# Three attention batches as one chain of head pairs, with products with v for six tiles at a time

## The chip, the cores and the metric

The kernel runs on one core of a Trainium2 chip. A core has five engines that run side by side, each working through its own instructions in order: TensorE (PE in the profile: matrix products and transposes; its weight loads are listed as PEld), VectorE (DVE), ScalarE (ACT), GpSimd (POOL) and SyncE (SP, which here only issues transfers). The metric is the device time of one execution in microseconds; lower is better.

## The reference

Windowed attention with a bias by distance, followed by a mixture of four experts. Cut to what matters:

```python
# q, k, v: (4 batches, 8 heads, 768 positions, 64)
scores = q @ k.T / sqrt(64) - slope[head] * dist      # dist: distance in positions
scores = where(is_global | is_local, scores, -1e9)    # first 8 columns, and the 96 before a row
a = softmax(scores)
attn = a @ v
x = attn.transpose(0, 2, 1, 3).reshape(3072, 512)
p = domain_probs / domain_probs.sum(-1)
out = sum(p[:, e] * (relu(x @ w1[e]) @ w2[e]) for e in range(4))   # w1: 512x1024, w2: 1024x512
```

All of it is float32.

## The kernel before

**Batches and stages.** Batch 0's attention runs first and nearly alone. Then come the experts of batches 0 and 1 (functions `first` for x times w1 with ReLU, `second` for the product with w2), and between their steps, as a second stream of work, the attention of batches 1, 3 and 2. At the end the experts of batches 2 and 3 run together with no attention left (`late_batch`). The expert products split each float32 operand into a high and a low part and use a seven-product scheme on 2x2 blocks, so an expert unit is seven groups of six 384-column products (`pm<-xB,w1s`, `pm<-xT,w1s`) and six groups of six 512-column products (`pm<-w2s,h`). Their four PSUM banks `pm` come free only when VectorE, and for the first kind ScalarE too, has read them.

**One batch of attention.** Heads go in four pairs, in the order `PAIRS`. A pair has six query tiles of 128 rows. `prepare_q` and `prepare_k` transpose half a pair's q or k on TensorE (`pt<-ident,q`, `pt<-ident,k`) and split it into high and low. For q the ScalarE part (L340) and the VectorE part (L341) go to a tile `st_q`, and four transfers (L345 to L347) copy its two heads into both partition halves of `qd`, so that one product can use the high and the low part of k, stacked in `kd`. `scores` makes a tile's scores (`ps<-kd,qd`, four products), `softmax` works on VectorE and ScalarE (`pb`, `nmax`, `zsum`), `turn` transposes the weights (`pt<-ident,pb`, copied to `pT`), and `weigh` multiplies three tiles by v (`pt<-pT,v`, `pt<-pT,vg`; `vg` holds v shifted to the window of the tile before). `weigh`'s result is copied out of PSUM by ScalarE: to `x` for batches 1 and 2, and for batch 3 to a small tile `piece` that ScalarE then sends to DRAM (L493 to L495, `x_last<-piece`). The tile `piece` has one buffer.

**Steps.** A tile goes through scores, exponentials, division and transposes in consecutive calls of `flow` (L507), and after three finished tiles `weigh` is called. Each of the three batches is a generator of 53 steps: one for its loads, 12 for each pair, and 4 that empty the pipeline. The main loop (L1393 to L1395) takes a step at about every second expert step.

**What sets the order.** In this stage (`Ordered.on = False`) a scheduler at build time interleaves the two streams by priority and by when it thinks a buffer is free; on the chip the order on each engine is then fixed, with waits on semaphores. Buffer counts (L983 to L985) matter for that reason: `pt` has two PSUM banks, shared by the transposes and by `weigh`; `qd`, `nat` (natural q and k) and `natv` (natural v) have one buffer each. SP issues all loads and copies, in order as well, so a load that waits for a free buffer holds those behind it.

Of the kernel before, what the change touches and what calls it, by code (L numbers as in the profile page):

```python
# [10 lines left out]
F32 = mybir.dt.float32  # L11
# [176 lines left out]
def attn_moe_kernel(ctx: ExitStack, tc, q, k, v, n_global, n_local, domain_probs, w1, w2, out):  # L188
# [95 lines left out]
    class Pools:  # L284


        def __init__(self, stack, name, st, kd, qd, nat, natv, pb, ps, pt, px, early, side="left"):
            self.early = early

            def sbuf(part, bufs):  # L290
                return stack.enter_context(tc.tile_pool(name=f"{name}_{part}", bufs=bufs, side=side))

            def psum(part, bufs):
                return stack.enter_context(tc.tile_pool(name=f"{name}_{part}", bufs=bufs, space=PSUM))

            self.st, self.natv = sbuf("st", st), sbuf("natv", natv)
            self.kd, self.qd, self.nat, self.vg = sbuf("kd", kd), sbuf("qd", qd), sbuf("nat", nat), sbuf("vg", kd)
            self.pb, self.pT, self.small = sbuf("pb", pb), sbuf("pT", 4), sbuf("small", pb)
            self.ps, self.pt = psum("ps", ps), psum("pt", pt)

            self.px, self.pxname = (psum("px", px), "px") if px else (self.pt, "pt")
# [197 lines left out]
    def attention(b, A, early=False):  # L499


        x = xs[b] = None if b == B - 1 else xp.tile([P, NPAIR, S], F32, name="x")
        if x is None:
            xd[b] = dp.tile([P, NPAIR, S], F32, name="x_last")
        tiles, turned, ahead = [None] * 4, [], [None]

        def flow(new=None):  # L507

            one, two, three, four = tiles
            if new:  # L510
                if not early:
                    new["ps"] = scores(A, new["t"], gots[new["pr"]])
                elif new["t"] % 2 == 0:
# [5 lines left out]
            ready = len(turned) == TPH  # L519
            if ready and not early:  # L520
                weigh(A, turned, x, b)
            if three and not early:
                turn(A, three)
            softmax(A, one, two)
            if three and early:
                turn(A, three)
            if ready and early:
                weigh(A, turned, x, b)
            if ready:
# [6 lines left out]

        def prepare(nat, got):

            got["v"] = nat
            prepare_q(A, nat["q"], 0, got)  # L540
            yield 1
            prepare_k(A, nat["k"], 0, got)
            yield 1
            prepare_q(A, nat["q"], 1, got)
            yield 1
            prepare_k(A, nat["k"], 1, got)
            yield 1
            nat["vg"] = windows(A, nat["v"])
            yield 1
            yield 1  # L550
# [17 lines left out]
        if early:  # L568
            halves = [load(A, src, b, 0, n, 2) for n, src in (("q", q), ("k", k))]
            bias = biases(start_stack.enter_context(tc.tile_pool(name="setup", bufs=1)))  # L570
            next(bias)
            nats[0] = dict(zip(("q", "k"), (next(h) for h in halves)))
            for h in halves:
                next(h)
            nats[0]["v"] = next(load(A, v, b, 0, "v"))
            todo = [prepare_all(pr) for pr in PAIRS]
            next(bias)
            next(todo[0])
            start(PAIRS[1])
        else:  # L580
            start(0)
            yield
        for m, pr in enumerate(PAIRS):
            cur = gots[pr]
            if not early:
                prep = prepare(nats[pr], cur)
                for _ in range(3):
                    next(prep)
                    flow()
                    yield  # L590
            for t in range(NQT):
                if early:
                    if t == 2 and m + 2 < NPAIR:
                        start(PAIRS[m + 2])
                elif t in (1, 2, 3):
                    next(prep)
                    flow()
                    yield
                if t == NQT - 1 and not early and m + 1 < NPAIR:
                    start(PAIRS[m + 1])  # L600
                flow({"t": t, "pr": pr, **cur})
                if early:
                    if (m, t) in BIASES:
                        next(bias)
                    for _ in range(AHEAD[m][t]):
                        while todo and next(todo[0], 0) == 0:
                            todo.pop(0)
# [4 lines left out]

# [348 lines left out]
    with ExitStack() as start_stack:  # L961
        A = Pools(start_stack, "start", st=1, kd=2, qd=2, nat=2, natv=3, pb=4, ps=2, pt=3, px=1, early=True)
        for n, _ in enumerate(attention(0, A, early=True)):
# [20 lines left out]
        att_stack, "att", st=1, kd=1, qd=1, nat=1, natv=1, pb=2, ps=2, pt=2, px=0, early=False, side="right"  # L984
# [367 lines left out]
    count, span = 3 * (NPAIR * (6 + NQT) + 5), (LATE * 13 * per - 12) * 0.97  # L1352
# [4 lines left out]
    att = chain(attention(1, A), attention(3, A), attention(2, A))  # L1357
# [87 lines left out]
```

## Time and profile before

| | us |
|---|---|
| median of 3 runs | 1180.61 (1180.2 to 1181.75) |
| the profiled execution's own time | 1180.03 |
| its span, first to last instruction | 1178.2 |
| of it 84 to 665, where experts and the three batches of attention share the engines | 581 |

The profile comes from one execution, 0.6 us below the median of the runs. PE is listed as busy for 98% of the span. In the profile's instruction lists a matrix product's end is modelled, so products overlap on paper; the time that one really costs TensorE is the distance from its start to the next one's start. A float32 product with v appears as two records. The helper that records instructions has one line, L44, so groups are told apart by tiles.

### The profile page before, as it was taken

The numbers are of one execution on the slowest core, as the hardware profiler recorded it, in microseconds if no ns is written. First come the engines' busy times: TensorE is split into PE (matmuls) and PEld (weight loads), VectorE is DVE, ScalarE is ACT, GpSimd is POOL, SyncE is SP. The second block draws the span as 40 slices with busy tenths as digits, with TensorE's granted clock in tenths as the row PEclk, the third lists the DMA queues.
The fourth block names the chain that finished last, engine by engine and source line by source line (L and its number), as shares of the span: only waits on it lengthen the run. The fifth ranks groups of instructions, "written<-read, shape, count | busy, mean of one in ns | idle before, by whom it ended". The sixth has DMA issues, their size and how long they took to land.

```text
span 1178.2 us, 21209 instructions
## 1 busy us (share of the span) xinstructions
PE 1149.0 (98%) x7488; PEld 1063.7 (90%) x7488; DVE 839.0 (71%) x1923; ACT 610.0 (52%) x1588; POOL 598.2 (51%) x584
## 2 busy tenths in 40 slices
PE   7789999999999999999999999999999999999997
PEld 5579898998898988888898889999999999999997
DVE  7876677676668677667666677777777777777776
ACT  6864767774743555455455434444444544444443
POOL 5776446455341222410420437777767855555554
PEclk9899999999999999999999999999999999999999
DMA  9578887886889899987897858888888687767764
GB/s 192 164 239 272 274 254 260 252 288 226 248 312 288 282 287 261 274 268 224 276 271 230 285 190 323 293 310 301 297 296 296 226 300 252 251 235 256 255 218 130
DMA packets 185201, 305.09 MB, mean 259 GB/s; under 512 B 87168, under 2 KB 137344, under 8 KB 172672
## 3 DMA queue, kind: packets, MB, share of 16 engines
q1 hardware_dynamic: 181488, 298.15, 77.8%
q10 hardware_dynamic: 3600, 5.51, 1.3%
q8 instruction: 62, 1.02, 0.4%
q14 instruction: 51, 0.42, 0.1%
HBM read 209.24 MB, written 70.78 MB: 238 GB/s over the span
## 4 chain that ended last, share of the span: by engine, by line
PE 87%; DVE 4%; DMA 3%; ACT 3%; issue 1%; POOL 1%; SPq 0%; DVEq 0%; ACTq 0%; POOLq 0%
PE pm L44 39%; PE pf L44 19%; PE X L44 11%; PE Y L44 9%; PE pt L44 6%; PE ps L44 3%; DMA qd<-st_q 2%; ACT pb L44 1%; DVE pb L44 1%; DMA raw<-in_moe_w_dram 1%; DMA out_dram<-acc 1%; POOL w1s L44 0%; DVE hA L44 0%; ACT pT L44 0%; SPq L44 0%
## 5 line engine op out<-in xcount | busy, mean ns | idle before, releaser
L44 PE MATMUL pm<-w2s,h 128*128 128x512 f32 x1152 | 288.4, 398 | 2.8 <-DVE h L44 2.8
L44 PEld LDWEIGHTS pm<-w2s,h 128*128 128x128 f32 x1152 | 209.6, 188 | 45.1 <-DVE h L44 3.9
L44 ACT ACTIVATE hf<-pf 128x384 f32<-128x384 f32 x128 | 62.8, 492 | 248.2 <-DVE pf L44 247.0
L44 POOL TENSOR_TENSOR hS<-sf,hS 128x384 fp32r<-128x384 f32 x126 | 133.5, 1077 | 112.9 <-ACT hS L44 112.2
L44 DVE SCALAR_TENSOR_TENSOR acc<-pm,prob,acc 128x512 f32<-128x512 f32 x180 | 133.7, 748 | 63.6 <-PE pm L44 62.5
L44 POOL TENSOR_TENSOR sums<-raw 128x256 f32<-128x256 f32 x54 | 39.2, 744 | 262.8 <-DMA raw<-in_moe_w_dram 183.2
L44 PE MATMUL pm<-xT,w1s 128*128 128x384 f32 x768 | 153.8, 341 | 0.7 <-DVE h L44 0.7
L44 PE MATMUL pf<-xT,w1s 128*128 128x384 f32 x768 | 146.5, 335 | 0.7 <-ACT hf L44 0.5
L44 PEld LDWEIGHTS pm<-xT,w1s 128*128 128x128 f32 x768 | 132.6, 188 | 3.2 <-DVE h L44 1.0
L44 PEld LDWEIGHTS pf<-xT,w1s 128*128 128x128 f32 x768 | 131.3, 188 | 1.5 <-ACT hf L44 1.0
L44 DVE TENSOR_TENSOR hA<-hf,hA 128x384 fp32r<-128x384 f32 x94 | 84.6, 925 | 50.5 <-ACT hA L44 50.5
L44 ACT ACTIVATE pb<-pb,nmax 128x256 f32<-128x256 f32 (+1 forms) x192 | 93.6, 493 | 46.9 <-DVE nmax L44 46.3
L44 PE MATMUL pm<-xB,w1s 128*128 128x384 f32 x570 | 115.5, 340 | 0.6 <-ACT x L44 0.6
L44 PE MATMUL pf<-xB,w1s 128*128 128x384 f32 x576 | 110.8, 335 | 0.1
L44 PEld LDWEIGHTS pm<-xB,w1s 128*128 128x128 f32 x570 | 98.7, 188 | 4.2 <-issue 1.4
L44 ACT ACTIVATE h<-pm 128x384 fp32r<-128x384 f32 x128 | 61.5, 489 | 73.8 <-DVE pm L44 72.5
L44 PEld LDWEIGHTS pf<-xB,w1s 128*128 128x128 f32 x576 | 98.7, 188 | 0.6 <-ACT hf L44 0.3
L44 POOL TENSOR_TENSOR sf<-hf 128x384 f32<-128x384 f32 x63 | 70.4, 1118 | 43.7 <-ACT hf L44 43.7
L44 DVE CUSTOM_DVE_ANT_0 pb<-ps,nbias 128x256 f32<-128x256 f32 (+1 forms) x192 | 71.4, 396 | 9.0 <-PE ps L44 8.2
L44 DVE SCALAR_TENSOR_TENSOR h<-pm,h 128x384 fp32r<-128x384 f32 x128 | 69.8, 551 | 8.4 <-ACT h L44 7.3
L44 PE MATMUL X<-w2b,hS 128*128 128x256 f32 x576 | 74.0, 282 | 0.0
L44 PE MATMUL Y<-w2b,hS 128*128 128x256 f32 x576 | 73.9, 282 | 0.0
(148 smaller groups left out, 2163.6 us busy)
## 6 DMA issues: line engine op xcount, KB each, us to landing
w1s<-kept SPq DMA_DIRECT2D x48, 1792.0 KB, 8.6
w2b<-kept SPq DMA_DIRECT2D x224, 256.0 KB, 4.1
kept<-w1s SPq DMA_DIRECT2D x16, 1792.0 KB, 9.8
raw<-in_moe_w_dram SPq DMA_DIRECT2D x43, 512.0 KB, 5.8
qd<-st_q SPq DMA_DIRECT2D x96, 192.0 KB, 3.8
kept<-w2s SPq DMA_DIRECT2D x16, 1024.0 KB, 7.0
w2s<-kept SPq DMA_DIRECT2D x16, 1024.0 KB, 6.6
v<-in_v_dram SPq DMA_DIRECT2D x16, 384.0 KB, 4.9
```

Of the source, the lines that this page charges most:

```text
L44: ins = fn(*args, **kwargs)
```

## The change

The second attention generator is written anew. Batch 0's (`attention_early`) is the old code with the other branch taken out. The other three batches become one generator, `attention_chain`, over twelve (batch, pair) items: the pipeline is no longer emptied between batches, and there are 149 steps in place of 159, spread over the same expert steps. `prepare_q` writes its high and low parts straight to the head's own half of `qd` (two ScalarE and two VectorE instructions on 64 partitions each) and copies each to the other half with one transfer. `weigh` is called twice in a row when six tiles have gathered. q and k of the next pair are requested at tile 2, v of the current pair right after the weighing of the pair before. `qd` gets two buffers and `pT` six (in `Pools`, for this stage alone).

```diff
-            self.pb, self.pT, self.small = sbuf("pb", pb), sbuf("pT", 4), sbuf("small", pb)
+            self.pb, self.pT, self.small = sbuf("pb", pb), sbuf("pT", 4 if early else 6), sbuf("small", pb)
...
         tp = transpose_half(A, nat, hf)
-        st = A.st.tile([P, 2, HALF], F32R, name="st_q")
-        ac.activation(st[:, 0, :], tp[:, :HALF], AF.Copy, scale=-SCALE)
-        ve.scalar_tensor_tensor(
-            st[:, 1, :], tp[:, :HALF], -SCALE, f32(st[:, 0, :]), op0=ALU.mult, op1=ALU.subtract
-        )
         qd = got[("q", hf)] = A.qd.tile([P, 2, 2, HALF], F32R, name="qd")
         for j in range(2):
-            for n in range(2):
-                sy.dma_start(f32(qd[n * D : (n + 1) * D, j]), f32(st[j * D : (j + 1) * D]))
+            own = slice(j * D, (j + 1) * D)
+            ac.activation(qd[own, j, 0], tp[own, :HALF], AF.Copy, scale=-SCALE)
+        for j in range(2):
+            own, oth = slice(j * D, (j + 1) * D), slice((1 - j) * D, (2 - j) * D)
+            ve.scalar_tensor_tensor(
+                qd[own, j, 1], tp[own, :HALF], -SCALE, f32(qd[own, j, 0]), op0=ALU.mult, op1=ALU.subtract
+            )
+            sy.dma_start(f32(qd[oth, j]), f32(qd[own, j]))
...
+    def attention_chain(bs, A):
+
+        tiles, turned = [None] * 4, []
+        order = [(b, pr) for b in bs for pr in PAIRS]
+        nats, gots = [{} for _ in order], [{} for _ in order]
+
+        def flow(new=None):
+
+            one, two, three, four = tiles
+            if new:
+                new["ps"] = scores(A, new["t"], gots[new["m"]])
+            if four:
+                turned.append(four)
+            if len(turned) == NQT:
+                b = order[four["m"]][0]
+                for half in (turned[:TPH], turned[TPH:]):
+                    weigh(A, half, xs[b], b)
+                turned.clear()
+            if three:
+                turn(A, three)
+            softmax(A, one, two)
+            tiles[:] = [new, one, two, three]
...
+        fetch_heads(0, "qkv")
+        yield
+        for m, (b, pr) in enumerate(order):
...
+            nat, got = nats[m], gots[m]
+            for part, hf in ((prepare_q, 0), (prepare_k, 0), (prepare_q, 1)):
+                part(A, nat[part.__name__[-1]], hf, got)
+                flow()
+                yield
+            for t in range(NQT):
+                if t in (1, 2, 3):
+                    if t == 1:
+                        prepare_k(A, nat["k"], 1, got)
+                    elif t == 2:
+                        fetch_heads(m + 1, "qk")
+                    else:
+                        nat["vg"] = windows(A, nat["v"])
+                    flow()
+                    yield
+                flow({"t": t, "pr": pr, "m": m, "v": nat})
+                if t == 0 and m:
+                    fetch_heads(m, "v")
+                yield
...
-        att_stack, "att", st=1, kd=1, qd=1, nat=1, natv=1, pb=2, ps=2, pt=2, px=0, early=False, side="right"
+        att_stack, "att", st=1, kd=1, qd=2, nat=1, natv=1, pb=2, ps=2, pt=2, px=0, early=False, side="right"
...
-    count, span = 3 * (NPAIR * (6 + NQT) + 5), (LATE * 13 * per - 12) * 0.97
+    count, span = 3 * NPAIR * (6 + NQT) + 5, (LATE * 13 * per - 12) * 0.97
...
-    att = chain(attention(1, A), attention(3, A), attention(2, A))
+    att = attention_chain((1, 3, 2), A)
```

Outside of the stretch in which the three batches run, every engine's instructions keep their order. Inside it they move; three places are shown. The first is TensorE, in batch 3, where a pair's first scores are followed by the products with v of the pair before. `weigh` of three tiles, before:

```order
L44 MATMUL ps<-kd,qd 128x256 x4
L44 MATMUL pt<-pT,vg 64x128 x2
L44 MATMUL pt<-pT,v 64x128 x2
L44 MATMUL pt<-pT,vg 64x128 x2
L44 MATMUL pt<-pT,v 64x128 x2
L44 MATMUL pt<-pT,vg 64x128 x2
L44 MATMUL pt<-pT,v 64x128 x2
L44 MATMUL pm<-w2s,h 128x512 x12
```

And the same place, second pair of batch 3, now:

```order
L43 MATMUL ps<-kd,qd 128x256 x4
L43 MATMUL pt<-pT,v 64x128 x2
L43 MATMUL pt<-pT,vg 64x128 x2
L43 MATMUL pt<-pT,v 64x128 x2
L43 MATMUL pt<-pT,vg 64x128 x2
L43 MATMUL pt<-pT,v 64x128 x2
L43 MATMUL pt<-pT,vg 64x128 x2
L43 MATMUL pt<-pT,v 64x128 x2
L43 MATMUL pt<-pT,vg 64x128 x2
L43 MATMUL pt<-pT,v 64x128 x2
L43 MATMUL pt<-pT,vg 64x128 x2
L43 MATMUL pt<-pT,v 64x128 x2
```

The three batches had 28 separate runs of such products on TensorE (24 calls of `weigh`, three of them cut into two or three by expert products or transposes); now there are 12, each of 22 products, none of them cut.

The second place is ScalarE at the same pair. The names in brackets are the semaphores that an instruction waits for: PE, DVE, or one of eight DMA lanes (DMAHW0 to 7). Before, the first half's `piece` is sent, and the second half's copy stands 17 rows below the first's (not shown):

```order
L44 COPY piece<-pt 128x384 [waits PE_49]
L44 ACTIVATE pb<-pb,zsum 128x256
L44 DMA x_last<-piece 128x384 [waits DMAHW6_49,Activation_49]
L44 ACTIVATE st_q<-pt 128x384 [waits DMAHW4_49,PE_49]
L44 COPY pT<-pt 128x512 [waits PE_49]
L44 ACTIVATE pb,zsum<-pb,nmax 128x256 [waits DVE_49] x2
L44 ACTIVATE zsum<-zsum 128x2 [waits Activation_49]
```

Now the two halves are close together:

```order
L43 COPY piece<-pt 128x384 [waits DMAHW1_49,PE_49]
L43 ACTIVATE pb,zsum<-pb,nmax 128x128 [waits DVE_49]
L43 DMA x_last<-piece 128x384 [waits DMAHW6_49,Activation_49]
L43 ACTIVATE zsum<-zsum 128x2 [waits Activation_49]
L43 ACTIVATE pb<-pb,zsum 128x128 [waits DVE_49]
L43 ACTIVATE pb<-pb,zsum 128x128
L43 ACTIVATE h<-pm 128x384 [waits DVE_49]
L43 COPY piece<-pt 128x384 [waits DMAHW6_49,PE_49]
L43 CAST kd<-pt 64x3x128 [waits PE_49]
L43 DMA x_last<-piece 128x384 [waits DMAHW1_49,Activation_49]
L43 ACTIVATE h<-pm 128x384 [waits DVE_49]
```

The second copy of `piece` moved up: it is the fifth instruction behind the first one's transfer, and it waits for that transfer's lane, DMAHW6. An expert's ReLU (`h<-pm`) is among those behind it.

The third place is SP, where the copies of q are issued for one pair of batch 3, with the load of the next pair's q (`q<-in_q_dram`). Before (two halves of the pair, with other transfers between):

```order
L44 DMA qd<-st_q 64x768 [waits DMAHW6_49,DMAHW1_49,DVE_49]
L44 DMA w2s<-kept_0_2_2118 128x2048 [waits DMAHW2_49,PE_49]
L44 DMA qd<-st_q 64x768 [waits DMAHW3_49]
L44 DMA qd<-st_q 64x768 [waits DMAHW4_49]
L44 DMA qd<-st_q 64x768 [waits DMAHW5_49]
L44 DMA v<-in_v_dram 128x12x64 [waits DMAHW7_49,PE_49,Pool_49]
L44 DMA q<-in_q_dram 128x6x64 [waits DMAHW0_49]
L44 DMA q<-in_q_dram 128x6x64 [waits DMAHW1_49]
L44 DMA w1s<-kept_2_1_2215 128x3584 [waits DMAHW2_49,PE_49]
L44 DMA qd<-st_q 64x768 [waits DMAHW4_49,DMAHW3_49,DMAHW5_49,DVE_49,PE_49]
L44 DMA qd<-st_q 64x768 x2
```

Now:

```order
L43 DMA qd<-qd 64x768 [waits DMAHW4_49,DVE_49]
L43 DMA qd<-qd 64x768 [waits DMAHW5_49,DVE_49,Activation_49]
L43 DMA w2s<-kept_0_2_2105 128x2048 [waits DMAHW6_49,PE_49]
L43 DMA q<-in_q_dram 128x6x64 [waits DMAHW7_49,PE_49]
L43 DMA qd<-qd 64x768 [waits DMAHW0_49,DVE_49]
L43 DMA qd<-qd 64x768 [waits DMAHW1_49,DVE_49,Activation_49]
L43 DMA q<-in_q_dram 128x6x64 [waits DMAHW2_49]
L43 DMA v<-in_v_dram 128x12x64 [waits DMAHW4_49,PE_49,Pool_49]
```

A half's q now takes two transfers, and the second half's no longer wait for PE, that is, for the scores that read the one buffer before.

## Rows read from the trace of the kernel before

**Rows 1.** Busy us by engine in one stretch; then clock, DMA share, GB/s.

```profile
84.00:665.00 581.00, 575.62 (x3490) 513.09 (x3491) 401.26 (x952) 335.55 (x906) 213.66 (x212) 1.00 0.84 267
```

**Rows 2.** What PE waited for in 84:700: us, times, longest.

```profile
PE pm L44 <- DVE h L44: 2.8, 3, 1.5
PE ps L44 <- DMA qd<-st_q: 2.4, 4, 1.0
PE ps L44 <- ACT kd L44: 0.9, 1, 0.9
PE pt L44 <- ACT pT L44: 0.4, 2, 0.2
```

**Rows 3.** The same for 294:304, second half of a pair's q.

```profile
PE ps L44 <- DMA qd<-st_q: 1.4, 2, 1.0
```

**Rows 4.** PE's timeline, expert products undisturbed: start, length, count; idle before.

```profile
93.58 3.28 PE L44 MATMUL pm<-xT,w1s 128*128 128x384 f32 x18
...
99.82 8.33 PE L44 MATMUL pm<-w2s,h 128*128 128x512 f32 x36
...
107.99 1.22 PE L44 MATMUL pm<-xB,w1s 128*128 128x384 f32 x6
```

**Rows 5.** PE's timeline around one run of products with v.

```profile
586.49 0.68 PE L44 MATMUL pm<-xB,w1s 128*128 128x384 f32 x3
587.10 0.44 PE L44 MATMUL pt<-pT,vg 128*64 128x128 f32 x4
587.37 0.39 PE L44 MATMUL pt<-pT,v 128*64 128x128 f32 x4
...
588.24 0.39 PE L44 MATMUL pt<-pT,v 128*64 128x128 f32 x4
588.56 0.79 PE L44 MATMUL pm<-xB,w1s 128*128 128x384 f32 x3
589.19 0.34 PE L44 MATMUL pm<-xT,w1s 128*128 128x384 f32 x1
589.37 0.49 PE L44 MATMUL pt<-ident,k 128*128 128x128 f32 x3
589.61 0.42 PE L44 MATMUL pm<-xT,w1s 128*128 128x384 f32 x1
589.87 0.64 PE L44 MATMUL ps<-kd,qd 128*128 128x256 f32 x4
590.35 1.93 PE L44 MATMUL pm<-xT,w1s 128*128 128x384 f32 x10
```

**Rows 6.** Tile piece over the span: durations in ns; time to landing.

```profile
L44 ACTq DMA_DIRECT2D x_last<-piece x8: 326/336/352, 312.7 to 488.2; - x8
...
DMA to landing us min/median/max: 2.2/5.8/7.2
```

**Rows 7.** Tile piece in windows 320:330, 400:410, 444:452, 482:490, in turn.

```profile
DMA to landing us min/median/max: 5.7/5.7/5.7
...
DMA to landing us min/median/max: 4.3/4.3/4.3
...
DMA to landing us min/median/max: 3.9/3.9/3.9
...
DMA to landing us min/median/max: 6.0/6.0/6.0
```

**Rows 8.** Instruction groups, ACT and DVE: busy us, mean ns | idle before.

```profile
L44 ACT ACTIVATE h<-pm 128x384 fp32r<-128x384 f32 x128 | 61.5, 489 | 73.8 <-DVE pm L44 72.5
...
L44 ACT CAST kd<-pt 64x384 fp32r<-64x384 f32 x48 | 22.6, 471 | 15.4 <-PE pt L44 14.6
...
L44 ACT ACTIVATE pb<-pb,nmax 128x128 f32<-128x128 f32 x32 | 12.7, 401 | 17.3 <-DVE nmax L44 17.2
...
L44 DVE SCALAR_TENSOR_TENSOR h<-pm,h 128x384 fp32r<-128x384 f32 x128 | 69.8, 551 | 8.4 <-ACT h L44 7.3
...
L44 DVE TENSOR_TENSOR kd<-pt,kd 64x384 fp32r<-64x384 f32 x48 | 26.7, 555 | 15.0 <-ACT kd L44 13.5 <-PE pm L44 1.1
```

More of the change, by code (lines that the diff above doesn't have):

```diff
@@ L2 @@
 from contextlib import ExitStack
-from itertools import chain
 import concourse.bass as bass
@@ L497, in attn_moe_kernel, with attention_early @@
     xs, xd = {}, {}
[L499 to L504, printed above, removed]
+    def attention_early(A):
+        b = 0
+        x = xs[b] = xp.tile([P, NPAIR, S], F32, name="x")
         tiles, turned, ahead = [None] * 4, [], [None]
@@ L510, in flow @@
             if new:
-                if not early:
-                    new["ps"] = scores(A, new["t"], gots[new["pr"]])
-                elif new["t"] % 2 == 0:
+                if new["t"] % 2 == 0:
                     new["ps"], ahead[0] = scores_early(A, new["t"], gots[new["pr"]])
@@ L518, in flow @@
                 turned.append(four)
-            ready = len(turned) == TPH
-            if ready and not early:
+            softmax(A, one, two)
+            if three:
+                turn(A, three)
+            if len(turned) == TPH:
                 weigh(A, turned, x, b)
[L522 to L529, printed above, removed]
                 turned.clear()
@@ L535, in start @@
             nats[pr] = {n: next(load(A, src, b, pr, n)) for n, src in (("q", q), ("k", k), ("v", v))}
[L537 to L550, printed above, removed]
         def prepare_all(pr):
@@ L567, in attention @@
         nats, gots = {}, [{} for _ in range(NPAIR)]
[L568 to L582, printed above, removed]
+        halves = [load(A, src, b, 0, n, 2) for n, src in (("q", q), ("k", k))]
@@ L583, in attention @@
+        bias = biases(start_stack.enter_context(tc.tile_pool(name="setup", bufs=1)))
+        next(bias)
+        nats[0] = dict(zip(("q", "k"), (next(h) for h in halves)))
+        for h in halves:
+            next(h)
+        nats[0]["v"] = next(load(A, v, b, 0, "v"))
+        todo = [prepare_all(pr) for pr in PAIRS]
+        next(bias)
+        next(todo[0])
+        start(PAIRS[1])
         for m, pr in enumerate(PAIRS):
             cur = gots[pr]
[L585 to L588, printed above, removed]
+            for t in range(NQT):
+                if t == 2 and m + 2 < NPAIR:
+                    start(PAIRS[m + 2])
+                flow({"t": t, "pr": pr, **cur})
+                if (m, t) in BIASES:
+                    next(bias)
+                for _ in range(AHEAD[m][t]):
+                    while todo and next(todo[0], 0) == 0:
+                        todo.pop(0)
+                yield
@@ new lines, in attention_early, with fetch_heads @@
+        while any(tiles):
+            flow()
[15 more added lines that the diff above has]
+                turned.clear()
+            if three:
+                turn(A, three)
+            softmax(A, one, two)
+            tiles[:] = [new, one, two, three]
+        def fetch_heads(m, names):
+            if m < len(order):
+                for n in names:
+                    nats[m][n] = next(load(A, {"q": q, "k": k, "v": v}[n], *order[m], n))
+        fetch_heads(0, "qkv")
+        yield
+        for m, (b, pr) in enumerate(order):
+            if pr == PAIRS[0]:
+                xs[b] = None if b == B - 1 else xp.tile([P, NPAIR, S], F32, name="x")
+                if b == B - 1:
+                    xd[b] = dp.tile([P, NPAIR, S], F32, name="x_last")
+            nat, got = nats[m], gots[m]
[3 more added lines that the diff above has]
+                yield
+            for t in range(NQT):
+                if t in (1, 2, 3):
[5 more added lines that the diff above has]
+                        nat["vg"] = windows(A, nat["v"])
@@ L589, in attention @@
                     flow()
                     yield
[L591 to L607, printed above, removed]
+                flow({"t": t, "pr": pr, "m": m, "v": nat})
@@ L962, in attn_moe_kernel @@
         A = Pools(start_stack, "start", st=1, kd=2, qd=2, nat=2, natv=3, pb=4, ps=2, pt=3, px=1, early=True)
-        for n, _ in enumerate(attention(0, A, early=True)):
+        for n, _ in enumerate(attention_early(A)):
             if n == 9:
```

## The prediction

> **What bounds the kernel now.** I read the stretches first, then what TensorE waits for, then its timeline, then the transfers. Every engine's order is unchanged outside the stretch of the three attention batches, so only that stretch can pay or cost: 581 us of the span [rows 1]. The reader should see there that TensorE is busy for 575.6 of the 581 us, VectorE for 401 (69%) and ScalarE for 336 (58%), at a granted clock of 1.00. So TensorE is the bound, and a change can win only in two ways: by its 5.4 us of idle time, or by making the same products cost it less. The waits say who owns the idle time [rows 2]: 3.7 us belong to attention (scores waiting for the copies of q, 2.4 us in four places, or for kd, 0.9; transposes for pT, 0.4), and 2.8 us are expert products waiting for VectorE's h, which the change does not aim at. A wait costs somewhat more than its idle time, because the modelled end of the product ahead covers some of it.
>
> **What a run of products with v costs beside its products.** Undisturbed, 36 products of 384 columns take 99.82 - 93.58 = 6.24 us, 0.173 each, and 36 of 512 take 8.17, 0.227 each [rows 4] (the rows left out between are two more groups of 384 columns, 18 in all). In the timeline of one run [rows 5], three 384-column products last 0.61 us before the run starts, 0.09 more than 3 x 0.173. Inside the run four records take 0.22 (from 587.37 to 588.24 four such groups, 0.87), but the first four take 0.27 and the last four 0.32, together 0.15 more. The three products behind it take 0.63, which is 0.11 over. So entering and leaving costs 0.35 us, and none of it depends on the run's length. TensorE is not idle by any row of waits in that time; it is a cost inside "busy".
>
> **The change, part by part.**
> 1. *Fewer runs.* The order has 28 runs of these products in the three batches before and 12 after, with as many products. 16 x 0.35 = **-5.6 us**, all on TensorE and so all on the path. From both sides: -3.0 if only entry and exit of the run itself were saved and the product behind cost the same (16 x 0.19), -5.6 if all.
> 2. *Copies of q.* Two transfers in place of four, and a second buffer, so that the second half's copies no longer wait for the scores of the first half. The waits on copies, kd and pT come to 3.7 us, and some 0.16 more for each of the seven under the modelled ends: 4.8 us in all. Second halves' part, 1.4 us of idle time in two waits [rows 3] and 0.3 with what the ends hide, goes surely: they are now prepared before the pair's first scores, with a buffer of their own. The rest are first halves, whose copies are issued as far ahead of their scores as before, but which end with one transfer less per head. I take **-3.5 us** (from -1.7 to -4.8).
> 3. *Two half-width instructions in place of one.* A 64-partition instruction takes as long as one on all partitions: 0.47 against some 0.5 on ScalarE, 0.555 on VectorE [rows 8]. 24 more of each are 11 us of ScalarE and 13 us of VectorE, spread over 581 us at 58% and 69% busy. They lie beside TensorE's expert products. Where cover is gone it is the PSUM bank of a transposed q that comes free some 0.5 us later each. I take **+0.5 us** (0 to 2).
> 4. *Pipeline emptied once, loads in another order, step count.* The ten steps that go held no TensorE work. q and k are asked for four steps earlier, v just after its buffer is free, so SP no longer stands before a load. No cost. New small waits of a new order, which no row shows, I count **+1.0 us** (0 to 3).
> 5. *Batch 3's pieces: the new wait.* `piece` has one buffer. Before, the two halves were sent many microseconds apart; no row has ScalarE waiting for a landing. Now both are ready at once, and the second copy stands on ScalarE until the first has landed. Behind it in ScalarE's queue are a kd copy, a transfer and an expert's ReLU, VectorE's h waits for that ReLU, and TensorE's product after next waits for the PSUM bank that this h frees. Worked out for three of the four pairs, from the start of the pair's first scores: TensorE does scores (0.48 [rows 5]), 22 products with v (44 records, 2.4, and 0.24 around them), two groups of six at 1.04 and 0.11 after the run, transposes of k and the product behind them (0.24 + 0.09), six more of 384, six of 512 (1.37), scores (0.48) and six of 512: it comes for the bank after **9.9 us**. ScalarE copies the first piece when the first half is weighed, at 1.9; then 0.47 for the copy, an exponential of 0.4 with its accumulator, and the issue, so the transfer starts at about 3.3. After landing come copy 0.47, kd 0.47, issue 0.34, ReLU 0.49, h 0.55: 2.3 us [rows 6, 8]. TensorE therefore stands still for the landing time less 4.3 us (9.9 - 3.3 - 2.3). Landing took 2.2 to 7.2 us, 5.8 at the median [rows 6]: nothing at one end, 4 x 2.9 = 11.6 us at the other, 4 x 1.5 = 6.0 at the median. The nearest rows are the four transfers that, like the new one, start just as a pair's v is loaded: 5.7, 4.3, 3.9 and 6.0 [rows 7], which give 1.4 + 0 + 0 + 1.7. I take **+3.0 us**. The first pair's order differs a little and leaves TensorE somewhat more room.
>
> For that transfer the Trainium skill (DMA: Bandwidth & Descriptors, section Anatomy of one DMA — SWDGE (gpsimd) path) gives a fixed part of about 2 us and the bytes at 436 GB/s, fitted on GpSimd's path. By it a piece of 196,608 bytes would land in an estimated 2.5 us and this term would be nothing, the sum 3 us lower; the trace has one such landing, of 2.2 us, and a median of 5.8, and I go by the trace.
>
> **Sum:** -5.6 - 3.5 + 0.5 + 1.0 + 3.0 = **-4.6 us**, from the profiled execution's 1180.03 to 1175.4. The median of the runs is 0.6 higher, so **1176.0 us**.
>
> **The rivals.**
> - *A, a wash.* ScalarE's hold comes at the median landing in all four pairs (+6.0), and first halves of q are as late as before, since their distance from issue to scores has not grown (only -1.7): -5.6 - 1.7 + 6.0 + 1.5 = +0.2, 1180.8 us. For it: the median itself, and three of the five waits on scores are not second halves'. Against it: the nearest four landings, and shorter q copies.
> - *B, slower: ScalarE's hold.* Landings of batch 3's first halves near 7.2 us, with the same small gains on q: -5.6 - 1.7 + 11.6 + 1.5 = +5.8, 1186.4 us. It decides where the four holds come to 8.2 us, from landings of some 6.4 us on. For it: one landing took 7.2 [rows 6], and the 16 DMA engines are busy for 84% there [rows 1]. Against it: it was of a half without a load of v beside it, and there are 48 transfers fewer.
> - *C, no hold.* Landings stay under 4.4 us, as three of eight did (2.2, 3.9, 4.3): the fifth term is nothing, -7.6, 1173.0 us. The landing that the page gives would be this case.
> - *D, the run costs nothing of its own.* If the 0.35 us were the price of the first products with v rather than of a change between two kinds of product, merged runs would pay it again at the joint: the sum is +1.0, 1181.6 us. Against it: inside the run no group pays more than 0.22, also where v and vg alternate.
>
> **How the numbers follow.** Forecast 0.38 (its own range 1174 to 1178), C 0.20, A 0.22, B 0.15, D 0.05. A measurement of this kernel tells 0.2%, 2.4 us, from no change: faster is below 1178.2, slower above 1183.0. Forecast and C fall on the faster side: 0.58. A, half of D and the near edge of B lie within: 0.26. The rest of B and D: 0.16. The range for 8 in 10 runs from 1171.5 (C with all of the waits on q gone) to 1183.0, which leaves out most of B.
>
> **What would show it.** In the profile after, TensorE's timeline has runs of 44 records with v, some 2.6 us each, and groups of four inside at 0.22, at the joint too: else term 1 is wrong. The waits no longer list scores for copies of q, or under 1 us: else term 2. ScalarE's waits list `piece` for its own transfer, four times, and TensorE's list `pm` for VectorE's h or acc in the same places, 0 to 2 us each: if ScalarE waits for 4 us there and TensorE not at all, the chain behind it has more room than I counted; if TensorE waits for more than 2, rival B. Busy time of ScalarE and VectorE in the stretch rises by 11 and 13 us. The forecast is wrong if TensorE's idle time in the stretch is above 7 us, or if the stretch of batches 2 and 3 at the end, whose order is the same, changes its length.

## The result, and the profile after

The changed kernel takes 1168.18 us (median of 5 runs, 1167.88 to 1168.86) against 1181.2 us for the kernel before on the same chip (5 runs, 1180.2 to 1182.35): a ratio of 0.989, 95% interval 0.9876 to 0.9905. It is 13 us faster. The direction was foreseen; the size was not: 1176.0 had been forecast, and 1168.2 lies below the range. The profiled executions took 1180.03 and 1168.86 us, with spans of 1178.2 and 1167.0.

To see where the time went I set the traces side by side by the 544 VectorE instructions that read a `pm` bank, whose number and kinds are the same in all kernels here. Some of them change places with a neighbour, but the first and the last are the same instruction each time. The first starts at 68.4 us before and 67.6 after, the last at 702.6 and 690.9. Between the two, called the stretch below, the change saves 11.0 us. Behind the last one, 475.6 us were left before and 476.1 are left after, so the end stage kept its length, as forecast.

The stretch of [rows 1] in the changed kernel, with the same columns:

```profile
84.00:665.00 581.00, 578.93 (x3549) 525.39 (x3548) 422.68 (x985) 349.27 (x932) 216.42 (x213) 1.00 0.80 256
```

TensorE is still the bound, at the same clock, and its idle time fell from 5.4 to 2.1 us. That is 3.3 us of 11: most of the gain lies inside "busy". What TensorE waited for in 84:700, to be read against [rows 2]:

```profile
PE pm L43 <- DVE h L43: 1.1, 2, 0.8
PE pt L43 <- ACT pb L43: 0.8, 2, 0.4
```

No waits on copies of q, kd or pT are left. The fall of the waits for h from 2.8 to 1.1 is not a gain, though. The longest one before stands at the very edge of the window (first row, 84:100 in the kernel before), and the changed kernel has it too, a little earlier and so outside (second row, from TensorE's timeline):

```profile
PE pm L44 <- DVE h L44: 1.5, 1, 1.5
```

```profile
83.42 6.87 PE L43 MATMUL pm<-w2s,h 128*128 128x512 f32 x29 [1.44 <-DVE h L43]
```

One run of products with v on TensorE's timeline after (start, length, operation, count), in place of [rows 5]:

```profile
403.59 0.44 PE L43 MATMUL pt<-pT,v 128*64 128x128 f32 x4
403.86 0.39 PE L43 MATMUL pt<-pT,vg 128*64 128x128 f32 x4
...
404.73 0.39 PE L43 MATMUL pt<-pT,vg 128*64 128x128 f32 x4
404.95 0.39 PE L43 MATMUL pt<-pT,v 128*64 128x128 f32 x4
...
405.82 0.39 PE L43 MATMUL pt<-pT,v 128*64 128x128 f32 x4
406.14 1.33 PE L43 MATMUL pm<-xB,w1s 128*128 128x384 f32 x6
```

It has 44 records; the first four take 0.27 us, the last four 0.32, the others 0.22, also around the joint of the two calls of `weigh`.

The pieces of batch 3: landing times over the whole span against [rows 6], the four first halves (at 319, 405, 446 and 487 us) against [rows 7], and what ScalarE waited for in 300:500:

```profile
DMA to landing us min/median/max: 1.9/3.0/8.2
...
DMA to landing us min/median/max: 5.2/5.2/5.2
DMA to landing us min/median/max: 3.4/3.4/3.4
DMA to landing us min/median/max: 2.0/2.0/2.0
DMA to landing us min/median/max: 2.1/2.1/2.1
```

```profile
ACT piece L43 <- DMA x_last<-piece: 2.8, 2, 2.3
```

ScalarE waited for its own transfer in two places, not in four. The half-width instructions cost what [rows 8] said (groups as there):

```profile
L43 DVE SCALAR_TENSOR_TENSOR qd<-pt,qd 64x384 fp32r<-64x384 f32 x48 | 26.6, 555 | 6.4 <-ACT qd L43 4.7
L43 ACT ACTIVATE qd<-pt 64x384 fp32r<-64x384 f32 x48 | 23.3, 485 | 23.5 <-PE pt L43 23.0
```

Over the span VectorE is busy for 853.5 us in place of 839.0, and ScalarE for 622.3 in place of 610.0.

### The profile page after: what moved, and what is told of

Read it like the earlier page. It is cut to its first block, busy times and chain, and to the rows that moved or that the text cites. A ratio compares the mean times of both kernels' runs of the same rounds, so it can differ in the third digit from the quotient of the medians.

```text
span 1167.0 us, 21177 instructions
## 1 busy us (share of the span) xinstructions
PE 1139.2 (98%) x7488; PEld 1065.0 (91%) x7488; DVE 853.5 (73%) x1947; ACT 622.3 (53%) x1612; POOL 598.3 (51%) x584
## 4 chain that ended last, share of the span: by engine, by line
PE 87%; DVE 4%; ACT 4%; DMA 3%; issue 1%; POOL 1%; SPq 0%; ACTq 0%; DVEq 0%; POOLq 0%
PE pm L43 38%; PE pf L43 19%; PE X L43 11%; PE Y L43 9%; PE pt L43 6%; PE ps L43 3%; DMA raw<-in_moe_w_dram 1%; ACT pb L43 1%; DMA out_dram<-acc 1%; DVE pb L43 1%; POOL w1s L43 0%; DVE hA L43 0%; PE px L43 0%; DMA x_last<-piece 0%; DVE acc L43 0%
## 5 line engine op out<-in xcount | busy, mean ns | idle before, releaser
L43 PE MATMUL pm<-w2s,h 128*128 128x512 f32 x1152 | 281.4, 394 | 2.6 <-DVE h L43 2.6
```

What stands on the lines that cost most here:

```text
L43: ins = fn(*args, **kwargs)
```

## The experiments

All times are medians; the ratio is to the kernel before, run on the same chip. The last column is the length of the stretch of one profiled execution, less that of before. "Runs" are those of products with v in TensorE's order. The kernel before had medians of 1180.9 to 1181.8 on the four chips used, so a difference between two changed kernels by their medians is good to about 1 us.

| kernel | runs | us | ratio, 95% interval | stretch |
|---|---|---|---|---|
| changed kernel | 12 | 1168.2 | 0.9876 to 0.9905 | -11.0 |
| e6_bq: before, q written at once | 24 | 1175.1 | 0.9923 to 0.9961 | -4.1 |
| e9_bq_loads: e6, loads in the new order | 26 | 1176.7 | 0.9946 to 0.9978 | -3.2 |
| e1_three: changed, three tiles weighed | 24 | 1171.4 | 0.9887 to 0.9937 | -8.2 |
| e3_qd1: changed, one buffer qd | 25 | 1192.7 | 1.0063 to 1.0134 | +14.7 |
| e2_oldq: changed, q by the old way | 27 | 1179.6 | 0.9968 to 0.9996 | -2.7 |
| e5_bsix: before, six tiles weighed | 23 | 1185.5 | 1.001 to 1.0043 | +4.3 |
| e7_drain: changed, three chains | 14 | 1182.1 | 0.9988 to 1.0023 | +1.0 |
| e13_drain_st2: e7, two buffers of piece | 14 | 1176.5 | 0.9937 to 0.9972 | -4.6 |
| e4_st2: changed, two buffers of piece | 12 | 1167.1 | 0.9859 to 0.9899 | -12.5 |
| e8_hold: changed, pieces twice, portions | 12 | 1176.0 | 0.9944 to 0.9975 | -2.4 |
| e12_hold3: changed, first pieces four times | 12 | 1168.2 | 0.9857 to 0.9922 | -11.8 |
| e10_cut: changed, runs cut in six | 72 | 1192.5 | 1.0079 to 1.0115 | +12.6 |
| e11_front: its twin, runs whole | 12 | 1176.2 | 0.994 to 0.9972 | -3.3 |

### What a run costs: e1_three, e10_cut, e11_front

```diff
-            if len(turned) == NQT:
+            if len(turned) == TPH:
                 b = order[four["m"]][0]
-                for half in (turned[:TPH], turned[TPH:]):
-                    weigh(A, half, xs[b], b)
+                weigh(A, turned, xs[b], b)
```

> The changed kernel with three tiles weighed at a time again, and nothing else undone: TensorE's order then has 24 runs of products with v, each whole, in place of 12. Theory 1 (entering and leaving a run costs TensorE 0.35 us whatever its length): 12 x 0.35 = +4.2 us on the changed kernel's 1168.2, 1172.4 us, with no more waits on q than it has (none), and runs of 20 or 24 records of some 1.3 and 1.5 us. Theory 2 (the gain is the copies of q and the buffers, a run costs nothing of its own): 1168 to 1168.6 us.

It lost 3.2 us by the medians and 2.8 in the stretch, 0.23 to 0.27 per run. It has no hold on `piece`, however, as its halves are sent apart. Against e4_st2 below, which has none either, it is 4.3 us slower by both measures: 0.36 per run. Theory 2 is out. For a larger dose, e10_cut puts a transpose of the identity behind each tile's products; e11_front has the same 72 transposes ahead of its runs:

```diff
+            if not A.early:
+                te.transpose(px[:, HALF:], ident, ident)
         cols = slice((t - TPH + 1) * P, (t + 1) * P)
```

> The changed kernel with 72 added TensorE transposes of the identity (128 columns, into a part of the bank that nothing reads), one behind each tile's products with v, so that each run of 22 products is cut into six: 72 runs. To be compared with its twin, which has the same 72 transposes in front of the runs. Theory 1 (entering and leaving a run of products with 64-column weights costs 0.35 us, or the 0.23 that the run with three tiles gives): 60 more entries and exits, 14 to 21 us slower than the twin. Theory 2 (the price depends on what stands beside, and is paid only next to the expert products): 0 to 3 us slower than the twin.

> The twin: six added transposes of the identity in front of each of the 12 runs, which stay whole. 72 transposes at some 0.06 to 0.11 us each: 4 to 8 us slower than the changed kernel, 1172 to 1176 us, on both theories.

The twin is 8.0 us slower than the changed kernel, 0.11 per transpose. The cut kernel is 16.3 us slower than the twin (15.9 in the stretch): 0.27 us for each of 60 more entries and exits. TensorE's timeline inside a cut run, and the twin's six transposes and first group:

```profile
414.97 0.33 PE L43 MATMUL pt<-ident 128*128 128x128 f32 x1
415.23 0.44 PE L43 MATMUL pt<-pT,vg 128*64 128x128 f32 x4
415.50 0.39 PE L43 MATMUL pt<-pT,v 128*64 128x128 f32 x4
415.82 0.33 PE L43 MATMUL pt<-ident 128*128 128x128 f32 x1
```

```profile
406.55 0.82 PE L43 MATMUL pt<-ident 128*128 128x128 f32 x6
407.30 0.44 PE L43 MATMUL pt<-pT,v 128*64 128x128 f32 x4
```

The pattern of [rows 5] is there each time: 0.27 for the first four records, 0.32 for the last, and 0.26 from a transpose to the product with v behind it. A run costs 0.27 us next to transposes, and up to 0.36 next to expert products. The Trainium skill (TensorEngine Tiling (Array Packing), section Key Properties) says that a change of tiling mode makes TensorE drain. The trace agrees in so far as each such change costs time, here with a price, and in no row of waits; whether a drain is what costs it, no run shows.

### The copies of q: e6_bq, e3_qd1, e2_oldq

```diff
+++ e6_bq, in the kernel before: prepare_q of the changed kernel, and
-        att_stack, "att", st=1, kd=1, qd=1, nat=1, ...
+        att_stack, "att", st=1, kd=1, qd=2, nat=1, ...
+++ e3_qd1, in the changed kernel: qd=1; e2_oldq: qd=1 and prepare_q of the kernel before
```

> The kernel before with q written to its stacked tile at once, two transfers and two buffers; loads, three separate chains and weighing of three tiles as before. 24 runs of products with v in place of 28. Theory 1: 4 x 0.35 = -1.4, and -3.7 to -4.8 us of waits: 1174.8 to 1176 us of 1181.2. Theory 2 (all of the gain is here): 1168 to 1169 us. If the extra instructions of ScalarE and VectorE cost anything, it is slower by that (0 to 2 us).

> The changed kernel with one buffer for q's stacked tile in place of two. The scheduler then also makes 25 runs of products with v, some cut. Theory 1 (runs at 0.35 us each, and waits of scores on the second half's copies): 13 x 0.35 = 4.6, and 1.5 to 2.5 us of waits, 1174 to 1175.5 us. Theory 2 (only the waits count): 1169.7 to 1171 us. A third possibility, that the second buffer is worth nothing because the direct copies are short: 1172.8 us if runs cost, 1168.2 us if not.

> The changed kernel with q written as before, through the tile st_q and four transfers, and one buffer of the stacked tile; the loads, the single chain and the weighing of six tiles stay. The scheduler makes 27 runs of products with v. Theory 1: 15 x 0.35 = 5.3, and all of the 3.7 to 4.8 us of waits on q, kd and pT come back: 1177 to 1178.5 us; ScalarE and VectorE are busy for 11 and 13 us less. Theory 2: 1172 to 1173 us. If the single chain and the loads were worth something that I do not know of, it stays some us under 1177.

e6_bq came out as theory 1 had it, 6.7 us faster than the kernel before on its own chip (4.1 in the stretch). Four runs went by themselves, since the scheduler cuts none once there are two buffers; ScalarE's and VectorE's extra instructions cost nothing that shows. What TensorE waited for on q in 84:670:

```profile
PE ps L44 <- DMA qd<-qd: 1.5, 1, 1.5
...
PE ps L44 <- DVE qd L44: 0.3, 1, 0.3
```

e2_oldq lies 1 us above what theory 1 gave, but not by its terms alone: q's copies make TensorE wait for 1.4 us there, kd for nothing, and transposes wait 1.9 us for a `pt` bank that ScalarE's copies of `piece` and `pT` hold. e3_qd1 went far past every theory, 24.5 us slower than the changed kernel. Who waited for the scores and for q there, from the rows of tile `qd` in 84:700:

```profile
  PE ps L43: 14.3, 7
  ACT qd L43: 12.3, 8
```

ScalarE itself waits 12.3 us for scores: with the direct write, it can't begin the second half's q until the scores of the first half have read the only buffer, and everything behind it in its queue stands. The tile `st_q` of the kernel before had been a second buffer in disguise. So the direct write and the second buffer are one edit; the first alone is a loss. An estimated 5 of the 24.5 us come by another way. TensorE stood for 5.15 and 4.58 us on q's copies, and behind these waits its granted clock was 0.50 in 262:268 and 0.58 in 311:317, where the kernel before has 1.00 throughout: 0.50 is the lower of its two levels, 1.2 in place of 2.4 GHz. Its 512-column products then started 0.43 us apart in place of 0.227:

```profile
262.00:268.00 6.00, 5.93 (x20) 5.29 (x21) 2.38 (x9) 1.54 (x4) 1.27 (x1) 0.50 0.50 195
```

```profile
262.07 0.77 PE L43 MATMUL ps<-kd,qd 128*128 128x256 f32 x2 [5.15 <-DMA qd<-qd]
```

### The single chain: e9_bq_loads, e7_drain, e5_bsix

e9_bq_loads differs from e1_three by three chains in place of one (and by `pT` with four buffers, not six):

```diff
+++ e9_bq_loads, in e6_bq
...
-                if t == NQT - 1 and not early and m + 1 < NPAIR:
-                    start(PAIRS[m + 1])
+                if t == 2 and not early and m + 1 < NPAIR:
+                    start(PAIRS[m + 1], "qk")
...
                 flow({"t": t, "pr": pr, **cur})
+                if t == 0 and m and not early:
+                    start(pr, "v")
...
+++ e7_drain, in the changed kernel
...
+    att = chain(*(attention_chain((b,), A) for b in (1, 3, 2)))
+++ e5_bsix, in the kernel before: pT 6 buffers, v requested as in e9, and
...
+                weigh(A, turned[:TPH], x, b)
+                weigh(A, turned[TPH:], x, b)
```

> The kernel before with q written at once, two buffers (1175.1 us by its own run), and the loads in the new order: q and k of the next pair at tile 2, v behind the weighing of the pair before. Three chains and weighing of three tiles as before; 26 runs of products with v, two of them cut short, in place of 24. Theory 1 (the loads' order is worth nothing by itself, since the one long wait on a copy of q stands at a batch's start, where loads are as before): 2 x 0.3 = +0.6, 1175 to 1176.5 us, and the wait of 1.5 us stays. Theory 2 (loads asked for earlier bring q earlier): 1173 to 1174 us.

> The changed kernel with its chain cut into three, one for each batch (159 steps again): the pipeline is emptied between batches, and a batch's first q, k and v are asked for only at its own first step. 14 runs of products with v in place of 12. Theory 1 (the single chain counts by its early loads): 2 x 0.3 = 0.6 us for the runs, and one or two waits of 1 to 2 us of the scores on the copies of q at the start of batch 3 or 2, as the kernel before with q written at once had one of 1.5 us at the start of batch 2: 1170 to 1172 us. Theory 2 (as the prediction had it, the steps that go are free): 1168.2 to 1169 us.

> The kernel before with six tiles weighed at once (six buffers for pT, v's load behind the weighing, since it could not come earlier), q through st_q and one buffer as before. The scheduler still makes 23 runs of products with v, against 28. Theory 1 (only the number of runs counts): 5 x 0.3 = -1.5 us, waits on q unchanged, 1179 to 1180 us. Rival (the weighing moves the waits on q too): more than 2 us either way.

The loads' order alone brings nothing (theory 1 of e9). The single chain does: e1_three is 5.3 us faster than e9_bq_loads, 5.0 in the stretch, of which two runs are some 0.6. The waits of e9 show part of it. At the start of batch 3 (275:285) and of batch 2 (495:510) TensorE waits, and the copies of q for the latter took 8.9 us to land (last row, tile `qd` in 492:493):

```profile
PE pm L44 <- DVE h L44: 0.4, 1, 0.4
```

```profile
PE ps L44 <- DMA qd<-qd: 1.6, 1, 1.6
```

```profile
DMA to landing us min/median/max: 8.9/8.9/9.0
```

e1_three has no wait in 480:510. There the copies were issued at 479.4, 8.5 us ahead of their scores, and took 5.0 us; in e9 they were issued 7.5 us ahead, 0.6 behind a weights' load of 1.8 MB (`w1s`) that landed at 500.8, just before them. In the kernel before, four of the five waits on q and kd stand in a batch's first pair as well (before the scores at 284.3, 302.1, 304.0 and 504.8). [rows 3] is two of them, 302.1 and 304.0. They are those of a second half in a first pair, and the second buffer alone took them away: e6 has none there, with three chains still. The other two are the start of a batch itself.

e7_drain was a surprise, 14 us slower than the changed kernel; the theories had 0 to 4. e5_bsix came out some 4 us slower than before, where theory 1 had it 1.5 faster: with one buffer the scheduler cuts the weighing again (23 runs), and TensorE's waits longer than 0.15 us sum to 10.8 us against 7.2 before. Behind one wait of 1.95 us its granted clock was 0.61 in 508:512, which by the starts' distances costs an estimated 1.6 us of the 4.

### The hold on piece: e13_drain_st2, e4_st2, e8_hold, e12_hold3

What TensorE waited for in e7_drain, in 320:460, and ScalarE's timeline at one of the places:

```profile
PE pm L44 <- DVE h L44: 5.0, 4, 2.8
PE pm L44 <- DVE acc L44: 0.9, 1, 0.9
```

```profile
447.98 0.33 ACTq L44 DMA_DIRECT2D x_last<-piece  x1
...
453.72 0.48 ACT L44 COPY piece<-pt 128x384 f32<-128x384 f32 x1 [4.68 <-DMA x_last<-piece]
...
454.60 0.96 ACT L44 CAST kd<-pt 64x384 fp32r<-64x384 f32 x2 [0.40 <-ACT piece L44]
455.58 0.49 ACT L44 ACTIVATE h<-pm 128x384 fp32r<-128x384 f32 x1
```

This is the fifth term of the prediction: ScalarE stands for 4.68 us on the second copy, what is behind it is late, and TensorE then waits 2.8 us for h. In this order the second copy stands ahead of every ReLU. The prediction let h wait for the ReLU alone. Here the delay also passes through VectorE's own queue: VectorE stands for ScalarE's kd copies, and the h that TensorE waits for comes two instructions behind:

```profile
455.59 1.12 DVE L44 TENSOR_TENSOR kd<-pt,kd 64x384 fp32r<-64x384 f32 x2 [3.48 <-ACT kd L44]
456.74 0.57 DVE L44 TENSOR_TENSOR pm<-pm,p 128x384 f32<-128x384 f32 x1
457.22 0.55 DVE L44 SCALAR_TENSOR_TENSOR h<-pm,h 128x384 fp32r<-128x384 f32 x1
```

A second buffer of `piece` takes it away, in e7 and in the changed kernel, with TensorE's order as it was:

```diff
...
+            self.pT0 = None if early else sbuf("pT0", 1)
...
+        if w0 and not A.early:
+            pT = A.pT0.tile([P, 1, 2, P], F32, name="pT0")
...
-        att_stack, "att", st=1, kd=1, qd=2, ...
+        att_stack, "att", st=2, kd=1, qd=2, ...
```

> The changed kernel cut into three chains as in the run before (1182.1 us, 14 us over the changed kernel), and two buffers for piece; TensorE's order is that of the run before. There ScalarE's second copy of piece stands ahead of the next ReLU, landings were 4.4 to 6.9 us, and TensorE's idle time in batch 3 was some 6.5 us at five places behind such a hold. Theory 1 (the hold of the prediction's fifth term is the larger part of the 14 us): 6 to 9 us faster than the run before, 1173 to 1176 us, with TensorE's waits for h and acc between 328 and 456 us gone; what is left against the changed kernel is the batch starts. Rival (the time is lost by the emptied pipeline itself): within 2 us of the run before.

> The changed kernel with two buffers for piece (the room for it comes from a smaller tile for the transposed weights of a pair's first tile), TensorE's order unchanged. ScalarE's waits for piece (2.8 us, in two places) go. Theory 1 (landings now are short, so nothing waits behind ScalarE's hold): no change, 1168.2 us, within 1 us. Rival (the hold still costs TensorE through late h): 1 to 3 us faster, and TensorE's waits for h shrink from 1.1 us.

e13 won back 5.7 us of the 14; instruction by instruction it has gained 7.3 us on e7 by the end of batch 3, and gives 1.7 back in batch 2. What TensorE still waited for in 320:460:

```profile
PE pm L44 <- DVE h L44: 0.3, 1, 0.3
PE ps L44 <- DMA qd<-qd: 0.2, 1, 0.2
```

So the hold was nearly half of e7's loss (5.7 of 14.0 us, 5.6 of 11.9 in the stretch). What is left is the three chains, without a hold: e13 is 9.4 us slower than e4_st2, which differs from it by the single chain and two runs fewer, and 7.9 in the stretch. By the distances between TensorE's starts 3.6 us of these lie at the first pairs of batches 3 and 2 (a wait of 2.0 for q's copies among them), as much at later pairs of batch 2, 0.7 at two runs and 0.6 elsewhere in batch 3; batch 1 gives 0.7 back. In the changed kernel the same edit gains 1.1 us by the medians and 1.5 in the stretch, 1.1 of it at batch 3's first pair. That gain is small against the interval, but e4_st2 is the fastest kernel here. Two runs lengthened the hold:

```diff
+++ e8_hold
+            twice = dp.tile([P, HALF // 32, 64], F32, name="twice")
+            ac.dma_start(twice[:, :, :32], piece.rearrange("p (a c) -> p a c", c=32))
             ac.dma_start(xd[b][:, pr, cols], piece)
+++ e12_hold3
+            if t < TPH:
+                for _ in range(3):
+                    more = dp.tile([P, HALF], F32, name=f"more{_}")
+                    ac.dma_start(more, piece)
             ac.dma_start(xd[b][:, pr, cols], piece)
```

> The changed kernel, TensorE's order unchanged, with every piece of batch 3 sent twice: first in 128-byte portions to a scratch area, then as before, so that ScalarE's hold on the second copy lengthens by the first transfer's time. Theory 1 (the chain of the prediction: TensorE stands still for the time from the first half's transfer to its landing, less 4.3 us, at each of four places): with 8 us it is some +15 us, 1183 us, with TensorE's waits named h or acc after ScalarE's piece in those places; with 5 us, +3 us. Rival (the queue behind the hold has other work that covers it): ScalarE waits for 4 us and more at each place, TensorE for none, 1168 to 1169 us.

> The changed kernel, TensorE's order unchanged, with the first half's piece of batch 3 sent four times as a whole, to three scratch places and then to its own, so that ScalarE's hold lengthens without small portions and without a slow issue. Theory 1 (TensorE stands still for the time from the first of these transfers to the last one's landing, less 4.3 us): with 6 us it is 1.7 us, with 8 us 3.7 us at each of four places, of which 1.6 at the first place are in the changed kernel already; its delay against the changed kernel at each place is that number within 0.7 us. Rival: no TensorE delay until the hold is 7 us or longer.

e8_hold lost 7.8 us, but for the most part not by my chain: in ScalarE's timeline the transfer behind the portions takes 5.49 us to issue at the third place and 5.26 at the fourth, and the ReLU stands behind that. Behind the fourth TensorE stood for 2.29 us, and its granted clock was 0.72 in 502:508, an estimated 1.6 us more. At the first place a hold of 4.0 us cost 1.7, by way of VectorE's kd copies.

```profile
454.19 0.52 ACTq L43 DMA_DIRECT2D twice<-piece  x1
454.75 5.49 ACTq L43 DMA_DIRECT2D x_last<-piece  x1
460.29 0.49 ACT L43 ACTIVATE h<-pm 128x384 fp32r<-128x384 f32 x1 [5.63 <-issue]
```

It does not tell the theories apart. e12_hold3 refutes theory 1 in the form I had given it: holds of 8.8, 6.6, 7.7 and 7.9 us, from the first issue to the last landing, should have cost 13.8 us, and cost nothing, although ScalarE waited for longer than in the changed kernel (11.3 us against 2.8):

```profile
ACT piece L43 <- DMA x_last<-piece: 11.3, 4, 3.5
```

Its timeline at the third place shows why. The scheduler put both ReLUs and both kd copies ahead of the second copy:

```profile
447.71 0.49 ACT L43 ACTIVATE h<-pm 128x384 fp32r<-128x384 f32 x1 [1.91 <-DVE pm L43]
...
448.45 0.47 ACT L43 CAST kd<-pt 64x384 fp32r<-64x384 f32 x1 [0.16 <-PE pt L43]
448.83 0.48 ACT L43 ACTIVATE h<-pm 128x384 fp32r<-128x384 f32 x1
449.34 0.48 ACT L43 CAST kd<-pt 64x384 fp32r<-64x384 f32 x1
...
453.26 0.48 ACT L43 COPY piece<-pt 128x384 f32<-128x384 f32 x1 [3.02 <-DMA x_last<-piece]
```

The room of 4.3 us belongs to one order of ScalarE's queue, and with the added transfers the scheduler made another. So no run lengthens the hold in the changed kernel's own order, and the formula itself was not put to a test there. What is shown is that holds of 6.6 to 8.8 us cost nothing where the ReLUs and the kd copies stood ahead of them.

## Why the prediction was right in direction and wrong in size

| term | predicted | measured | from |
|---|---|---|---|
| 1 fewer runs | -5.6 | -4.3 to -5.8 | 16 x 0.27 to 0.36 |
| 2 and 3, q and half-width | -3.0 | -2.7 to -5.6 | e6 (-4.1, -6.7) less four runs |
| 4 chain, loads, new waits | +1.0 | -4.3 to -4.8 | e1 less e9 (-5.0, -5.3), less two runs |
| 5 hold on piece | +3.0 | +1.1 to +1.5 | e4 |

The measured terms add up to between -9.8 and -15.1 us, around the -11.0 of the stretch and the -13.0 of the medians.

**The step that failed is the fourth**: "The ten steps that go held no TensorE work", "No cost", and +1.0 for small waits of a new order. The steps held none, but waits of TensorE at a batch's first pairs stand behind them, and with one chain they are gone. At the one followed to its cause it was the copies' landing, beside a large load, that changed. The rows had hinted at it, faintly: two of the waits on q and kd stand at the start of a batch (284.3 and 504.8), and I had not asked what they share. The new small waits do exist (0.8 us for pb) and are part of the measured sum. That is not the whole of the term, however. Laid side by side by the distances between TensorE's starts, the 5.0 us of the stretch between e9 and e1 lie 2.9 us at the first pairs of batches 3 and 2, 1.9 at later pairs of batch 2, where transposes and products with v wait for ScalarE's pb and pT, and 0.7 at the two more runs; batch 1 gives 0.9 back, and 0.4 is spread. So the single chain is shown to gain the 4.3 to 4.8 us, but the emptied pipeline is seen in only some 3 of them. The chain also takes 149 steps over the same expert steps in place of 159, so later pairs meet other expert work; e1 also has six buffers of `pT` and e9 four. No run takes these apart, and how the rest divides stays open.

**The fifth named a real mechanism, in part by the wrong chain, and had the wrong landing times.** At the first place the landing of 5.2 us gives 0.9 by the formula, and TensorE there waits 0.76 us for h. That the two are near is luck. The formula was worked out for the other three pairs; at the first no ReLU stands close behind the second copy, VectorE stands for 2.97 us on ScalarE's kd copies, and the h that TensorE waits for comes 12 us later, by way of the softmax:

```profile
326.24 1.12 DVE L43 TENSOR_TENSOR kd<-pt,kd 64x384 fp32r<-64x384 f32 x2 [2.97 <-ACT kd L43]
```

At the others the landings of 3.4, 2.0 and 2.1 us give nothing, and nothing is seen. I had taken 5.7, 4.3, 3.9 and 6.0 from transfers of the kernel before at about the same place in a pair. But the weights' load `w2s` (1 MB) had landed before the piece started in three of four places of the changed kernel; at the third it landed in 5.1 us, at 443.9, and the piece went at 446.4. In e7_drain it was still in flight, 8.6 us, to 451.4, and the piece that went at 448.0 took 5.7:

```profile
DMA to landing us min/median/max: 5.1/5.1/5.1
```

```profile
DMA to landing us min/median/max: 8.6/8.6/8.6
```

At the first place of the changed kernel a 1 MB write of kept weights was in flight. In these two kernels the pieces that were issued with a transfer of 1 MB or more already in flight took 4.4 to 8.2 us, the others 1.9 to 3.9. That is a correlation, and not a full one: in the kernel before one piece landed in 2.2 us beside such a write, and no run changes the neighbour alone. The estimate of 2.5 us, worked out from the Trainium skill's fit (DMA: Bandwidth & Descriptors, section Anatomy of one DMA — SWDGE (gpsimd) path), is near the 1.9 to 3.4 us of the changed kernel's pieces without such a neighbour, and far from the 5.2 of its first place.

**The first term** held, and with it the way of reading it: a price inside "busy" was taken from the distances of starts in [rows 5], at one run, and came out at 0.27 to 0.36 in three kernels. Its lower bound was worked out wrongly: without the product behind, the rows give 0.35 - 0.11 = 0.24 a run and -3.8, not 0.19 and -3.0; nothing else hung on it. Rival D is out: neither the joint nor a whole run of 44 pays again. **The second and third** held in size together; no run separates them. The cover for the half-width instructions was there: in e6 VectorE and ScalarE are busy for 13.7 and 13.2 us more than before (13 and 11 forecast; 14.5 and 12.3 in the changed kernel), and no cost of it shows. Rivals A and B fell with the landings, although B's mechanism is real: it is nearly half of e7_drain's loss. C was nearest, at 1173.0, and lacked the fourth term.

## What to carry to other kernels

Sort waits by place in the program before sorting them by what they wait for: waits that gather behind a loop's boundary can be the price of emptying the pipeline there, and joining the loops can take them away. A staging tile can be a second buffer in disguise, so a direct write into the destination needs another buffer of the destination. Before pricing an instruction that will wait for a transfer, list what stands behind it in its own queue and in the queues of the engines that wait for it, and which large transfers are in flight when its own starts.

## What the runs showed of the hardware beyond that

Switching TensorE between products with 64-column weights and those with 128 costs 0.27 to 0.36 us for going there and back, with no row of waits. A transfer of 192 KB landed in 1.9 us at best and in 8.2 at worst in the changed kernel; the slow ones there were issued while one of 1 MB or more was in flight, but no run changes that neighbour alone. Behind a stand of 5.15 us (e3_qd1) the granted clock of TensorE was 0.50. A second transfer issued from ScalarE right behind one made of 128-byte portions held that engine for up to 5.49 us in its issue, where 0.33 is usual.
